# Retention and a gated MLP on one core: each chunk from the fifth on loaded as two halves instead of as one transfer

## The chip, the cores and the metric

The kernel runs on one core of a Trainium2 chip. The metric is the device time of one execution in microseconds (us), as the median of several runs. A core has TensorE (matmuls, PE in the profile, with its weight loads as PEld), VectorE (DVE), ScalarE (ACT), GpSimd (POOL) and SyncE (SP). Each works through its own queue of instructions in order; semaphores order them against each other. In this kernel SP computes nothing: it issues the transfers between memory (HBM) and the core's SBUF, which 16 DMA engines carry out.

## What is computed

There are 4 batches, 8 heads, 768 tokens and 64 values per head. For each batch and head a state of 64 x 64 decays at every token and takes up the product of k and v; the output is q times the state. Over the 512 joined head values of each token runs a gated MLP: a causal convolution of 5 taps gives a gate, the gate multiplies a projection, and a second projection follows.

```
for t in range(S):
    state = gamma * state + k[:, :, t] (outer) v[:, :, t]
    y[:, :, t] = scale * (q[:, :, t] . state)
x = y with the heads joined                     # (B, S, 512)
gate = sigmoid(sum over k of conv_w[k] * x shifted by k tokens)
out = (gate * (x @ w_val)) @ w_out
```

All of it is in 32-bit floating point; the weights come as 64-bit words that the kernel converts itself.

## The kernel before, in words

**Chunks.** The 768 tokens are cut into 6 chunks of 128. A chunk here is one chunk of tokens of one batch, with all heads, so there are 24, numbered 0 to 23 in the order of `chunks`: the four batches' first chunks are 0 to 3. In memory a chunk is 128 partitions of four planes of 512 values: plane 0 is q by dimension, plane 1 is k by dimension, plane 2 is v by token, plane 3 is k by token. For chunks 0 to 3 plane 3 is not loaded but made on the chip (`turn`, `take`). A whole chunk of four planes is 1 MB, with 8 KB per partition. The tile `att` that holds it has four buffers (`LB = 4`), so chunk g + 4 goes into the buffer of chunk g.

**Work on a chunk.** `decay` (GpSimd, line 192) multiplies v in place by its decay; for chunks 0 to 3 it does this to k. `scores` (TensorE, line 201) multiplies k and q by dimension into PSUM, `mask` (VectorE, line 210) masks them into u, `state` (TensorE, line 222) adds the products of k and v by token to the state, in two halves of 64 tokens, and `snap` (ScalarE, line 232) copies the state out. `y_scores` multiplies u with v and `y_state` the state with q (both at line 342), and `evac` (VectorE, line 395) scales the result into x. For chunks 4 to 23 TensorE's part is `block`, which takes up chunk g and begins chunk g + 1, in this order: `y_scores(g)`, `state(g, 1)`, `state(g + 1, 0)`, `y_state(g)`, `scores(g + 1)`. The first of it, `first_block`, is `state(4, 0)` and then `scores(4)`.

**The MLP.** Weights are converted on ScalarE, VectorE and GpSimd into a high and a low part. Of x, too, a rounded part (`round_x`, ScalarE) and its rest (`rest_x`, GpSimd, line 408) are made. `val` (TensorE, line 537) and `outp` (line 565) are the two projections, with three products each. `tap` (line 521 on ScalarE, line 523 on VectorE) is the convolution. `store` (ScalarE, line 575) copies a result out of PSUM, `send` (SP, line 579) writes it to memory.

**Order.** Every piece of work is a `Step` with its engine, what it reads and what it writes. `steps` are sorted by their due times, and the list `TURNS` gives the order in which they are written out, by number; -1 stands for `fill`, a matmul on zeros that keeps TensorE busy. `plan` asserts that no step comes ahead of what it needs and that a buffer's users are all written out ahead of the first user of the next tile in it. What an engine does in which order is fixed by that list; when it does it is up to the semaphores. The loads are steps too: `load_at` makes them and `load` issues them on SP (line 180), with the sends and the weight loads (line 423) in the same queue.

Of the kernel before, what the change touches and what calls it, by code (L numbers as in the profile page):

```python
# [16 lines left out]
P = 128  # L17
# [30 lines left out]
def plan(steps, turns, fill):  # L48

    steps = sorted(steps, key=lambda s: s.due)  # L50
# [36 lines left out]
    return [steps[i] if i >= 0 else fill for i in turns]  # L87
# [3 lines left out]
def tile_retention_gated_mlp(  # L91
# [70 lines left out]
    steps = []  # L162
# [143 lines left out]
    def fill():  # L306
        nc.tensor.matmul(
            z_ps[:, 0].rearrange("p b j e -> p (b j e)"),
            lhsT=warm.broadcast_to([P, P]), rhs=warm.broadcast_to([P, 512]),
            start=not begun, stop=True, skip_group_check=True,  # L310
        )
# [270 lines left out]
    def first_sigmoid():  # L582
# [345 lines left out]
    with tc.manual_schedule():  # L928
        for step in plan(steps, TURNS, Step(0.0, "PE", 0.2345, [], [], fill, ())):
            step.fn(*step.args)  # L930
# [99 lines left out]
```

## Time and profile before

| | |
|---|---|
| median of 3 runs | 213.23 us (213.15 to 213.98) |
| span of the profiled execution, first to last instruction | 212.0 us |
| TensorE busy | 202.8 us (96%), weight loads 160.9 us |
| VectorE, ScalarE, GpSimd busy | 136.0, 110.0, 105.6 us |
| SP's transfers | 34.66 MB on one queue, 44.0% of the 16 engines' span |
| loads of chunks | 20 of 1 MB, 3 of 768 KB, one in pieces of 512 and 256 KB |

The page gives no time of the profiled execution but its span; the median of the runs is 1.2 us more. [...] A row of a timeline gives the start of a group, how long it lasts from its first start to its last end, the engine, the line, the operation and the tiles; where the engine was idle ahead of it, the idle time and what ended it stand in brackets. Matmuls overlap in TensorE, so that a group's own duration is longer than the distance to the next group's start.

### The profile page before, as it was taken

What the parts mean: (1) busy time and instruction counts of PE and PEld (TensorE: products, weight loads), DVE (VectorE), ACT (ScalarE), POOL (GpSimd) and SP (SyncE); (2) the same over time, 40 slices, a digit from 0 to 9 for tenths busy, and PEclk for the clock granted to TensorE, in tenths of its full rate; (3) what the DMA queues carried; (4) which work ended last, traced back from release to release, by engine and by line L of the source; (5) the groups of instructions that cost most, each with busy time, mean ns of one, the idle gap of its engine ahead of it and who ended that gap; (6) DMA issues with size and microseconds to landing.
All of it is one profiled execution on the core that took longest, in us unless ns stands there. A gap on an engine that the chain in (4) does not pass through costs nothing.

```text
span 212.0 us, 7499 instructions
## 1 busy us (share of the span) xinstructions
PE 202.8 (96%) x3322; PEld 160.9 (76%) x3325; DVE 136.0 (64%) x209; ACT 110.0 (52%) x228; POOL 105.6 (50%) x98
## 2 busy tenths in 40 slices
PE   8999679999899999999999999999999999999993
PEld 3688467687687888888888878788878778877783
DVE  2986899999989952369736782616768257680000
ACT  2367988779835845273533742526560664523321
POOL 1277679899982337922239651422820456041300
PEclk9999999999999999999999999999999999999998
DMA  6998998576800995619533370111110111111122
GB/s 213 374 401 295 416 417 313 187 274 206 306 17 3 356 351 202 242 52 370 195 135 107 145 237 16 51 54 53 53 45 4 49 53 49 49 49 49 53 99 99
DMA packets 8402, 35.18 MB, mean 166 GB/s; under 512 B 937, under 2 KB 1193, under 8 KB 5810
## 3 DMA queue, kind: packets, MB, share of 16 engines
q1 hardware_dynamic: 8352, 34.66, 44.0%
q8 instruction: 26, 0.43, 0.8%
q10 hardware_dynamic: 18, 0.04, 0.1%
q14 instruction: 6, 0.05, 0.1%
HBM read 28.41 MB, written 6.29 MB: 164 GB/s over the span
## 4 chain that ended last, share of the span: by engine, by line
PE 82%; DVE 9%; ACT 2%; DMA 2%; issue 2%; SPq 0%; DVEq 0%; ACTq 0%
PE mm L565 32%; PE mm L537 28%; PE sy L342 9%; DVE acc L523 3%; PE sy L201 3%; PE z_ps L222 3%; PE sy L245 3%; DMA att<-in_att_dram 2%; PE mm L301 2%; PE mm L332 1%; PE z_ps L320 1%; DVE top L472 1%; DVE acc L478 1%; DVE acc L466 1%; DVE rest L482 1%
## 5 line engine op out<-in xcount | busy, mean ns | idle before, releaser
L523 DVE SCALAR_TENSOR_TENSOR acc<-x,cw_sb,acc 128x512 f32<-128x512 f32 x96 | 69.4, 751 | 7.2 <-ACT acc L521 6.4
L557 POOL TENSOR_TENSOR gvl<-gate,gvh 128x512 fp32r<-128x512 f32 x24 | 31.0, 1292 | 49.7 <-ACT gvh L553 49.6
L565 PE MATMUL mm<-woh,gvh 128*128 128x512 f32 (+1 forms) x100 | 38.9, 393 | 0.0
L575 ACT COPY o_sb<-mm 128x512 f32<-128x512 f32 (+1 forms) x25 | 14.2, 569 | 46.9 <-PE mm L565 46.8
L565 PE MATMUL mm<-wol,gvh 128*128 128x512 f32 (+1 forms) x100 | 38.5, 387 | 0.0
L565 PE MATMUL mm<-woh,gvl 128*128 128x512 f32 (+1 forms) x100 | 38.4, 386 | 0.0
L546 DVE TENSOR_TENSOR gate<-mm,gate 128x512 f32<-128x512 f32 x24 | 16.6, 690 | 33.0 <-PE mm L537 30.3
L408 POOL TENSOR_TENSOR xl<-x,xh 128x512 fp32r<-128x512 f32 x24 | 30.5, 1286 | 10.7 <-ACT xh L404 10.7
L192 POOL TENSOR_TENSOR att<-att,first_sb 128x512 f32<-128x512 f32 x24 | 24.9, 1042 | 19.2 <-DMA att<-in_att_dram 13.3
L537 PE MATMUL mm<-xh,wvh 128*128 128x512 f32 x96 | 32.5, 413 | 1.4 <-ACT xh L404 1.0
L537 PE MATMUL mm<-xh,wvl 128*128 128x512 f32 x96 | 30.3, 399 | 0.8 <-issue 0.8
L537 PE MATMUL mm<-xl,wvh 128*128 128x512 f32 x96 | 30.3, 397 | 0.5 <-POOL xl L408 0.5
L530 ACT ACTIVATE gate<-acc 128x512 f32<-128x512 f32 x24 | 14.3, 597 | 17.3 <-DVE acc L523 11.1
L565 PEld LDWEIGHTS mm<-woh,gvh 128*128 128x128 f32 x100 | 18.7, 188 | 5.4 <-ACT o_sb L575 1.3
L537 PEld LDWEIGHTS mm<-xh,wvl 128*128 128x128 f32 x96 | 18.0, 188 | 5.6 <-issue 1.1
L537 PEld LDWEIGHTS mm<-xh,wvh 128*128 128x128 f32 x96 | 17.4, 188 | 6.3 <-ACT xh L404 1.1
L565 PEld LDWEIGHTS mm<-woh,gvl 128*128 128x128 f32 x100 | 18.8, 188 | 4.0
L537 PEld LDWEIGHTS mm<-xl,wvh 128*128 128x128 f32 x96 | 17.8, 188 | 5.1 <-POOL xl L408 1.2
L565 PEld LDWEIGHTS mm<-wol,gvh 128*128 128x128 f32 x100 | 18.8, 188 | 3.7
L395 DVE TENSOR_TENSOR x<-sy,dec 128x512 f32<-128x512 f32 x20 | 13.8, 688 | 10.3 <-PE sy L201 9.6
L553 ACT CAST gvh<-gate 128x512 fp32r<-128x512 f32 x24 | 14.9, 619 | 6.9 <-DVE gate L546 4.4
L232 ACT COPY snap<-z_ps 128x256 f32<-128x256 f32 x40 | 14.7, 373 | 6.2 <-PE z_ps L222 4.8
(65 smaller groups left out, 268.9 us busy)
## 6 DMA issues: line engine op xcount, KB each, us to landing
att<-in_att_dram SPq DMA_DIRECT2D x20, 1024.0 KB, 6.5
out_dram<-o_sb SPq DMA_DIRECT2D x23, 256.0 KB, 2.1
wst<-in_w_dram SPq DMA_DIRECT2D x7, 512.0 KB, 7.9
att<-in_att_dram SPq DMA_DIRECT2D x3, 768.0 KB, 8.9
first_sb<-in_first_dram SPq DMA_DIRECT2D x1, 568.0 KB, 3.7
att<-in_att_dram SPq DMA_DIRECT2D x1, 512.0 KB, 5.0
att<-in_att_dram SPq DMA_DIRECT2D x1, 256.0 KB, 6.7
out_dram<-o_sb SPq DMA_DIRECT2D x2, 128.0 KB, 1.8
```

The source lines that it names most:

```text
L192: nc.gpsimd.tensor_tensor(v, v, vd_sb[:, c, :].unsqueeze(2).broadcast_to([P, 8, HALF]), op=ALU.mult)
L232: nc.scalar.copy(sn, z_ps[:, :, b])
L342: return nc.tensor.matmul(sy[cols, h, off:off + HALF], lhsT=lhsT, rhs=rhs, start=start, stop=True, skip_group_check=True,)
L408: nc.gpsimd.tensor_tensor(xl[n, ct], xs[n][:, ct, :, HALO:], xh[n, ct].bitcast(F32), op=ALU.subtract)
L523: nc.vector.scalar_tensor_tensor(acc, x[:, :, k:k + P], cw_sb[:, m, k:k + 1], acc, op0=ALU.mult, op1=ALU.add,)
L530: nc.scalar.activation(gate[n, m], accs.pop((n, m)), AF.Sigmoid)
L537: nc.tensor.matmul(vps[n, m], lhsT=w[:, m, ct * P:(ct + 1) * P], rhs=xx[n, ct].rearrange("p b t -> p (b t)"), start=(i == 0), stop=(i == 3 ...
L546: nc.vector.tensor_tensor(gv, vps.pop((n, m)), gv, op=ALU.mult)
L553: nc.scalar.copy(gvs[n, m][0], gate[n, m])
L557: nc.gpsimd.tensor_tensor(gvl, gate.pop((n, m)), gvh.bitcast(F32), op=ALU.subtract)
L565: nc.tensor.matmul(ops[n, b, cs.start][:, 0:cs.stop - cs.start], lhsT=gg[:, b * P:(b + 1) * P], rhs=w[:, ct, cs], start=(i == 0), stop=(i ...
L575: nc.scalar.copy(o_sb[:, 0:step], ops.pop((n, b, cs.start))[:, 0:step])
```

## The change

A chunk of four planes, from chunk 4 on, is loaded by two transfers of 512 KB instead of one of 1 MB. The first brings planes 0 and 1 (q and k by dimension), the second planes 2 and 3 (v and k by token). On SP the second stands right behind the first. Each has a step of its own: the first writes what `scores` and `y_state` read, the second what `decay`, `state` and `y_scores` read. There are 20 steps more, so the numbers in `TURNS` change, and the list is written anew. Read out engine by engine, the new list has the order of the old one on TensorE, VectorE, ScalarE and GpSimd, with all 17 fillers in their places; on SP it has the old order with each chunk's load replaced by its two halves. `fill` gets a size, and a second, smaller filler (128 columns) is made that the list does not use.

```diff
-def plan(steps, turns, fill):
+def plan(steps, turns, fills):
...
-    return [steps[i] if i >= 0 else fill for i in turns]
+    return [steps[i] if i >= 0 else fills[-1 - i] for i in turns]
...
-    def fill():
+    def fill(size):
         nc.tensor.matmul(
-            z_ps[:, 0].rearrange("p b j e -> p (b j e)"),
-            lhsT=warm.broadcast_to([P, P]), rhs=warm.broadcast_to([P, 512]),
+            z_ps[:, 0].rearrange("p b j e -> p (b j e)")[:, 0:size],
+            lhsT=warm.broadcast_to([P, P]), rhs=warm.broadcast_to([P, size]),
             start=not begun, stop=True, skip_group_check=True,
         )
...
     TURNS = (
...
     )
...
-        pieces = PIECES_OF.get(g, ((0, 4 if g >= B else 3),))
+        pieces = PIECES_OF.get(g, ((0, 2), (2, 4)) if g >= B else ((0, 3),))
         for a, z in pieces[1:] if late else pieces[:1] if (2, g) in FIRST_LOADS else pieces:
             what = [k for k, i in zip(keys, (1, 2, 3)) if a <= i < z]
             at(due, "DMA", 0.63 * (z - a), [], what, load, g, slice(a, z))
...
-        for step in plan(steps, TURNS, Step(0.0, "PE", 0.2345, [], [], fill, ())):
+        for step in plan(steps, TURNS, [Step(0.0, "PE", 0.2345, [], [], fill, (n,)) for n in (512, 128)]):
             step.fn(*step.args)
```

## Rows read from the trace of the kernel before

**Rows 1.** The page, part 1: busy us of each engine (share of span), instructions.

```profile
PE 202.8 (96%) x3322; PEld 160.9 (76%) x3325; DVE 136.0 (64%) x209; ACT 110.0 (52%) x228; POOL 105.6 (50%) x98
```

**Rows 2.** The page, part 4: the chain that ended last, shares of the span.

```profile
PE 82%; DVE 9%; ACT 2%; DMA 2%; issue 2%; SPq 0%; DVEq 0%; ACTq 0%
```

**Rows 3.** That chain in order of time, 20 to 30 us: start, us, what.

```profile
25.71 0.60 ACT acc L521
...
26.34 0.76 DVE acc L523
```

**Rows 4.** The table of waits: who waited for whom, us in total, times, longest.

```profile
POOL att L192 <- DMA att<-in_att_dram: 13.3, 6, 4.7
...
PEld z_ps L222 <- POOL att L192: 1.0, 1, 1.0
...
PE mm L537 <- POOL xl L408: 0.5, 1, 0.5
```

**Rows 5.** Loads of `att` on SP: issue ns; chunk 4's landing; timeline.

```profile
L180 SPq DMA_DIRECT2D att<-in_att_dram x25: 327/328/1208, 1.2 to 122.0; - x25
...
DMA to landing us min/median/max: 6.6/6.6/6.6
...
15.69 2.91 SPq L180 DMA_DIRECT2D att<-in_att_dram  x2
```

**Rows 6.** Timeline of GpSimd: the decays of chunks 4, 5, 6 with 7, and 14.

```profile
22.51 1.04 POOL L192 TENSOR_TENSOR att<-att,first_sb 128x512 f32<-128x512 f32 x1 [0.76 <-DMA att<-in_att_dram]
...
25.59 1.05 POOL L192 TENSOR_TENSOR att<-att,first_sb 128x512 f32<-128x512 f32 x1
...
32.76 2.04 POOL L192 TENSOR_TENSOR att<-att,first_sb 128x512 f32<-128x512 f32 x2
...
73.73 1.04 POOL L192 TENSOR_TENSOR att<-att,first_sb 128x512 f32<-128x512 f32 x1 [3.43 <-DMA att<-in_att_dram]
```

**Rows 7.** Timeline of TensorE, 22 to 27 us: state and scores of chunk 4, first projection.

```profile
23.60 0.46 PE L222 MATMUL z_ps<-att 64*64 64x64 f32 x16 [0.72 <-POOL att L192]
23.88 0.65 PE L201 MATMUL sy<-att 64*64 64x64 f32 x32
25.49 0.50 PE L537 MATMUL mm<-xh,wvh 128*128 128x512 f32 x1 [0.96 <-ACT xh L404]
```

**Rows 8.** One stretch: its length, busy us by engine, granted clock, DMA share, GB/s.

```profile
21.20:31.80 10.60, 7.44 (x221) 5.73 (x219) 9.92 (x16) 9.41 (x21) 7.87 (x10) 1.00 1.02 416
```

**Rows 9.** Timeline of VectorE: chunk 4's mask and the tap behind it.

```profile
24.80 0.69 DVE L210 TENSOR_TENSOR u<-sy,tri_sb 128x512 f32<-128x512 f32 x1
...
26.34 0.76 DVE L523 SCALAR_TENSOR_TENSOR acc<-x,cw_sb,acc 128x512 f32<-128x512 f32 x1 [0.26 <-ACT acc L521]
```

**Rows 10.** Timeline of TensorE: the state matmuls of chunks 13 and 14.

```profile
76.74 0.65 PE L222 MATMUL z_ps<-att 64*64 64x64 f32 x32
```

**Rows 11.** Line 222: wait instructions on TensorE's queue, whole span, then 48.9 to 49.2 us.

```profile
L222 PEldq EVENT_SEMAPHORE  x16: 51/51/164, 22.3 to 149.1; - x16
...
L222 PEldq EVENT_SEMAPHORE  x1: 51/51/51, 49.0 to 49.0; - x1
```

**Rows 12.** Timeline of TensorE: state, product with the state and scores in one block.

```profile
49.04 0.65 PE L222 MATMUL z_ps<-att 64*64 64x64 f32 x32
49.50 0.65 PE L342 MATMUL sy<-att,snap 64*64 64x64 f32 x32
49.97 0.65 PE L201 MATMUL sy<-att 64*64 64x64 f32 x32
```

**Rows 13.** The page, part 6: the stores, KB each, median us from issue to landing.

```profile
out_dram<-o_sb SPq DMA_DIRECT2D x23, 256.0 KB, 2.1
...
out_dram<-o_sb SPq DMA_DIRECT2D x2, 128.0 KB, 1.8
```

**Rows 14.** SP's timeline and `att` landings, 22.5 to 24 us: chunk 7's load.

```profile
22.96 0.33 SPq L180 DMA_DIRECT2D att<-in_att_dram  x1
...
DMA to landing us min/median/max: 9.4/9.4/9.4
```

132 rows, old and new, of the table TURNS are left out of this document.

## The prediction

> **What bounds the kernel now.** I read the busy shares first [rows 1], then the chain that ended last, first by engine and then in order of time [rows 2, 3], then the waits that a load can cause [rows 4], and last the neighbourhood of each such wait on SP, PE, VectorE and GpSimd. The reader is to see in the first that TensorE is busy for 202.8 of 212.0 us, so that all its idle time is 9.2 us; in the second that 82% of the chain is TensorE and 9% VectorE, and that only 2% is a transfer. That 2% is the very first load, of chunk 0, which the change leaves alone. In the third the reader is to see that after the first four chunks the chain goes to ScalarE and VectorE (25.71 to 26.34 us here) and not through a transfer or GpSimd: the transfers of chunks 4 to 23 are nowhere on it.
>
> The waits say the same in another way. GpSimd's decay of v waits six times for a landing, 13.3 us in all, but TensorE has waited for a decay in the blocks only once, for 1.0 us on its weight side [rows 4]. So five of the six waits on GpSimd are spare time of GpSimd. The one that reaches TensorE is chunk 4's: SP issues that load at 15.69 us, it lands 6.6 us later, at 22.3 [rows 5]; the decay starts at 22.51 and takes 1.04 [rows 6]; TensorE starts the state of chunk 4 at 23.60 after 0.72 idle [rows 7].
>
> **Part 1: who reads the first half.** The first half (q and k by dimension) is read by the scores and by the product of q with the state; the second (v and k by token) by the decay, the state and the product of v. In a block the first state of the next chunk stands ahead of its scores on TensorE, and in the first block too. So for every one of the 20 chunks the second half is wanted before the first, and a first half that lands early (by about half of the transfer) is waited for by nobody. The worth of the earlier landing is 0 us. What matters is when the second half lands, compared with the whole chunk before.
>
> **Part 2: the second half's landing.** SP issues 20 transfers more. An issue takes 0.33 us (0.327 smallest, 0.328 median, 1.208 largest) [rows 5], so the second half is asked for some 0.38 us later than the whole was: one issue and the small gap behind it. The bytes are the same. Between 21.2 and 31.8 us, with loads queued one behind the other, the 16 DMA engines have a busy share of 1.02 and move 416 GB/s [rows 8]: no gap shows between one queued transfer and the next, and 512 KB take 0.524 / 416 = 1.3 us (an estimate from that row). The first half's 1.3 us therefore cover the 0.38 us, and the second half should land when the whole did. The ends are 0 and 0.38 us of lateness where the cover holds; if the issue were as slow as the slowest one seen, 1.2 us. Earlier by up to 1.3 us is possible only if the first half is asked for earlier (the third rival). I take 0.1 us.
>
> What does lateness cost? At chunk 4 the decay and the state move with it at once: the state starts 0.05 us after the decay's end (22.51 + 1.04 = 23.55, against 23.60). Then there is slack. Its scores end at 23.88 + 0.65 = 24.53 and VectorE's mask starts only at 24.80, since VectorE is busy: 0.27 us. Behind the mask VectorE has 0.26 us idle before the tap at 26.34, which waits for ScalarE [rows 9]. TensorE itself next waits 0.96 us for ScalarE [rows 7]. So 0.27 + 0.26 = 0.53 us of lateness are absorbed at chunk 4 before the chain moves, and 0.1 or 0.38 us cost nothing. With 1.2 us it would cost 1.2 - 0.53 = 0.7 us. Of the other chunks whose decay waits for a landing, chunk 14 is the tightest: its decay starts at 73.73 [rows 6] and ends at 74.77, and the state is in the block whose state matmuls start at 76.74 [rows 10], 2.0 us later. Chunk 5's decay, at 25.59, waits for no landing.
>
> **Part 3: SP's queue.** Behind each load on SP stand other loads, weight loads and sends. Each is pushed back by 0.38 us per split load ahead of it, where SP is not waiting anyway. SP mostly waits: for TensorE to free a buffer, or for ScalarE's result. The largest pile is where three chunks are asked for behind the first send, 3 x 0.38 = 1.1 us for the send behind them; in the table of waits no row of TensorE, ScalarE or VectorE names a store. Without that cover a send could at most be 1.1 us late in mid-kernel; the sends at the end have no load ahead of them. Cost 0.
>
> **Part 4: one wait more per chunk on TensorE.** The scores now read data that no earlier instruction of TensorE has waited for, so each of 20 scores gains a wait that is long satisfied. The nearest row is the wait for a load ahead of the state: 16 separate wait instructions on TensorE's queue, 51 ns in the median [rows 11]. At one end each is paid in full, 20 x 0.051 = 1.0 us; at the other nothing. One of them, at 49.0 us, stands among the state's 32 matmuls of that block, and these take 49.50 - 49.04 = 0.46 us, while the next 32, with none, take 49.97 - 49.50 = 0.47 [rows 12]. So it is hidden by the matmuls in flight, and I take 0 to 0.01 us each, 0.1 us in all. The orders on TensorE, VectorE, ScalarE and GpSimd stay as they were, and the new size of the filler is never used, so the rewritten list by itself costs 0.
>
> **The sum.** 0 (part 1) + 0 (part 2, 0.1 us of lateness under 0.53 of slack) + 0 (part 3) + 0.1 (part 4) on the profiled execution's span of 212.0 us gives 212.1. The runs shown have a median of 213.23, 1.2 us more than that span; with the same 1.2 us around it, 213.3. That is the forecast; its own range is 212.9 to 213.9, and the change would not be visible: about 0.5% (1.07 us) is what a measurement of this kernel can tell from no change.
>
> **Rivals.** (1) *Each half pays a start of its own, and the second lands late (slower).* Stores of 128 and 256 KB land after 1.8 and 2.1 us [rows 13]: 0.3 us for the second 128 KB, so some 1.5 us of start (estimate). If that were not overlapped, chunk 4 would cost 1.5 - 0.53 = 0.97 us, 214.2. Four split loads follow each other there, and the lateness L of each adds up to chunk 7, which lands at 22.96 + 9.4 = 32.4 [rows 14]; its decay is the second of two from 32.76, so from 33.8 [rows 6], 1.4 us later. Late by 4 x 1.5 - 1.4 = 4.6 us it holds up the rounding remainders behind it on GpSimd, for which TensorE already waits 0.5 us [rows 4]: 217.9. It decides from 4L - 1.4 = 1.07, L = 0.6 us. Against it: the busy share of 1.02 [rows 8]. Chance 0.06. [...]
>
> (2) *The added waits are paid:* 1.0 us, 214.3. For it: TensorE has little idle time to hide them in. Against it: the 0.46 us above. Chance 0.05.
>
> (3) *The halves are freed apart (faster).* If the first half's buffer counts as free once the scores have read it, SP can ask for it earlier, and chunk 4's second half lands up to 1.3 us sooner. TensorE's wait there, 0.7 to 1.0 us, goes. But TensorE then waits longer for ScalarE, and the mask is held by VectorE; most likely nothing comes of it, 213.2. At the other end 1.0 us is gained, 212.2. Chance 0.07, for which nothing in this trace speaks directly.
>
> **The numbers.** Forecast 0.82; rivals 0.06, 0.05 and 0.07. Faster by over 0.5% lies at the far end of rival 3: 0.05. Slower by over 0.5% is rival 1 and a little of rival 2: 0.08. Within 0.5%: 0.87. The range, 212.5 to 214.2, takes in the 0.8 us between the runs shown, the 0.7 us of a slow issue and most of rivals 2 and 3, and leaves out rival 1's larger end.
>
> **What would show it.** Right: the 20 chunks stand as 40 issues of 512 KB; the second half of chunk 4 lands at 22.2 to 22.7; TensorE's wait for the decay there stays near 0.7 to 1.0 us; the four orders repeat nearly to the tenth; TensorE's busy time stays near 202.8. Wrong in part 2: chunk 4's decay starts after 23.0, or TensorE waits for a decay in more places than one. Wrong in part 4: the 32 scores take over 0.5 us. Rival 3: a first half is issued well before 15.69. What would make the whole wrong is a consumer that I have not seen to wait for q and k.

## The result and the profile after

| | before | after |
|---|---|---|
| median | 213.19 us (6 runs, 212.79 to 213.98) | 215.31 us (6 runs, 214.55 to 215.69) |
| ratio, 95% interval | | 1.0087 [1.0066, 1.0109] |
| profiled execution, span | 212.0 us | 212.8 us |
| granted clock, mean | 0.997 | 0.981 |

The change costs 2.1 us (0.9%), where I had said that it would not be seen. Time less span is 1.66 to 1.80 us in all executions of all kernels here, so the loss lies inside the span. The profiled execution of after is the fastest of its six runs (212.8 + 1.75 = 214.55), and it shows only part of the loss.

The page of after, the parts that answer to [rows 1, 2, 5]: busy us, queues, the chain by engine, loads with KB each and median us to landing.

```profile
PE 201.6 (95%) x3323; PEld 160.5 (75%) x3325; DVE 135.9 (64%) x209; ACT 109.6 (51%) x228; POOL 105.7 (50%) x98
...
q1 hardware_dynamic: 11232, 34.67, 46.3%
q8 instruction: 26, 0.43, 0.8%
...
PE 80%; DVE 6%; DMA 5%; issue 3%; ACT 2%; SPq 1%; POOL 1%; ACTq 0%
...
att<-in_att_dram SPq DMA_DIRECT2D x41, 512.0 KB, 5.7
```

The reader is to see that no engine works more, that the chain has 3% "issue" (2% before), and a queue that I had passed over: q8, "instruction", 26 packets with 0.43 MB, 16 KB each. It stands in the page of before with the same numbers. The chain's 5% DMA (2% before) is not the split loads here: it is one piece of 9.9 us that begins at 3.97 us, before the first of them is issued.

TensorE's timeline in after, three of the places where it stops:

```profile
25.15 0.49 PE L537 MATMUL mm<-xh,wvh 128*128 128x512 f32 x1 [1.63 <-ACT xh L404]
...
29.41 0.28 PE L222 MATMUL z_ps<-att 64*64 64x64 f32 x3 [2.25 <-issue]
...
57.98 0.50 PE L537 MATMUL mm<-xh,wvl 128*128 128x512 f32 x1 [0.73 <-issue]
```

The same view of before, two rows that front and prediction do not have:

```profile
28.38 0.28 PE L222 MATMUL z_ps<-att 64*64 64x64 f32 x3 [0.86 <-issue]
...
57.00 0.50 PE L537 MATMUL mm<-xh,wvl 128*128 128x512 f32 x1 [0.81 <-issue]
```

The stops marked "issue" wait for no tile and no semaphore that the profile shows. They stand in both kernels at the same instruction. (The stop of 1.63 us in after waits for ScalarE, as the one of 0.96 us does in [rows 7].)

GpSimd's timeline in after, the decays of chunks 4 to 7 and what follows them (compare [rows 6]):

```profile
21.49 1.04 POOL L192 TENSOR_TENSOR att<-att,first_sb 128x512 f32<-128x512 f32 x1
...
25.25 1.06 POOL L192 TENSOR_TENSOR att<-att,first_sb 128x512 f32<-128x512 f32 x1
...
32.38 1.06 POOL L192 TENSOR_TENSOR att<-att,first_sb 128x512 f32<-128x512 f32 x1
33.84 1.04 POOL L192 TENSOR_TENSOR att<-att,first_sb 128x512 f32<-128x512 f32 x1 [0.40 <-DMA att<-in_att_dram]
34.84 3.77 POOL L408 TENSOR_TENSOR xl<-x,xh 128x512 fp32r<-128x512 f32 x3
```

Chunk 4's decay waits for no landing and starts 1.0 us earlier than in before. That is not the change's doing: in the control below, the kernel before run again (e0), it starts at 21.50 us. But the decays of chunks 6 and 7, which were one group of two in [rows 6], are torn apart: chunk 7's second half is late, and the three rounding remainders (L408) start behind it.

### The profile page after: what moved, and what is told of

Its sections match the earlier page's. It is cut to its first block, busy times and chain, and to the rows that moved or that the text cites. A ratio compares the mean times of both kernels' runs of the same rounds, so it can differ in the third digit from the quotient of the medians.

```text
span 212.8 us, 7529 instructions
## 1 busy us (share of the span) xinstructions
PE 201.6 (95%) x3323; PEld 160.5 (75%) x3325; DVE 135.9 (64%) x209; ACT 109.6 (51%) x228; POOL 105.7 (50%) x98
## 3 DMA queue, kind: packets, MB, share of 16 engines
q1 hardware_dynamic: 11232, 34.67, 46.3%
## 4 chain that ended last, share of the span: by engine, by line
PE 80%; DVE 6%; DMA 5%; issue 3%; ACT 2%; SPq 1%; POOL 1%; ACTq 0%
PE mm L565 32%; PE mm L537 29%; PE sy L342 8%; DMA att<-in_att_dram 5%; PE sy L201 3%; PE z_ps L222 3%; DVE acc L523 1%; PE z_ps L320 1%; PE sy L245 1%; SPq L180 1%; DVE gate L546 1%; PE mm L301 1%; DVE x L395 1%; DVE u L210 1%; DVE top L472 1%
## 5 line engine op out<-in xcount | busy, mean ns | idle before, releaser
L408 POOL TENSOR_TENSOR xl<-x,xh 128x512 fp32r<-128x512 f32 x24 | 30.5, 1288 | 10.5 <-ACT xh L404 10.5
L537 PE MATMUL mm<-xh,wvh 128*128 128x512 f32 x96 | 33.2, 424 | 1.6 <-ACT xh L404 1.6
L537 PE MATMUL mm<-xh,wvl 128*128 128x512 f32 x96 | 30.9, 405 | 0.7 <-issue 0.7
L537 PEld LDWEIGHTS mm<-xh,wvh 128*128 128x128 f32 x96 | 18.1, 195 | 6.3 <-ACT xh L404 1.8
L537 PEld LDWEIGHTS mm<-xh,wvl 128*128 128x128 f32 x96 | 18.5, 192 | 5.4 <-issue 1.0
```

The costliest lines, as they stand in the source:

```text
L408: nc.gpsimd.tensor_tensor(xl[n, ct], xs[n][:, ct, :, HALO:], xh[n, ct].bitcast(F32), op=ALU.subtract)
L537: nc.tensor.matmul(vps[n, m], lhsT=w[:, m, ct * P:(ct + 1) * P], rhs=xx[n, ct].rearrange("p b t -> p (b t)"), start=(i == 0), stop=(i == 3 ...
```

## Experiments

All kernels are the kernel before with the edit shown, so that its line numbers hold. Most change only line 180, where SP issues a load; only e8 to e10 and e12 to e14 touch what TensorE issues. The medians of the kernel before that were measured beside them are 213.15 to 213.32 us. Below, "the code theory" means: TensorE's program comes in pieces of 16 KB (the 26 packets of q8, whose time the page counts on the same 16 DMA engines as the loads', 0.8% of their span), and a piece that is asked for behind queued loads comes late.

### e0 and e1: the control, and the halves alone

e0 is the kernel before, unchanged.

> The kernel before, unchanged, as a control. Both theories: ratio 1.000, within 0.2%. The code-block theory: TensorE's stop in the middle of the state matmuls of chunk 5, put down to issue (0.86 us in the profile of before), lasts 0.5 to 1.2 us here too, since the 16 KB block of TensorE's code that it waits for is fetched behind the loads in flight from 21 us on.

Measured: 213.5 us, ratio 1.0025 [1.0005, 1.0045]. The same kernel differs from itself by a quarter of a per cent; smaller differences below carry no weight. In its traced execution TensorE has one "issue" stop, at 57 us:

```profile
56.53 0.50 PE L537 MATMUL mm<-xh,wvl 128*128 128x512 f32 x1 [0.68 <-issue]
```

The stop near 28 us, expected to last 0.5 to 1.2 us, is not there: a miss. It comes and goes between executions of the same kernel.

```diff
# e1
-        nc.sync.dma_start(out=tiles[g][:, part], in_=att[i, :, part])
+        [nc.sync.dma_start(out=tiles[g][:, a], in_=att[i, :, a])
+         for a in ((slice(0, 2), slice(2, 4)) if g >= B else (part,))]
```

> The kernel before with its old list, in which each load from chunk 4 on issues two halves: the change without the rewritten list. Code-block theory and the theory of a cost per added transfer: as slow as the changed kernel, ratio 1.007 to 1.011. A theory that the rewritten list costs something: 1.000. Code-block theory: the stop in the state of chunk 5 lasts over 1.8 us.

Measured: 215.22 us, 1.0101 [1.0083, 1.012], as after. So the loss is made by the two transfers; the new list, the steps of their own and the finer waits add nothing to it. Its stop near 28 us lasted 0.54 us, not over 1.8: a second miss on that stop. Its profiled execution, 215.98 us, is the slowest of its five and shows the loss at 105 us, which after's, the fastest of six, does not have; TensorE in e1:

```profile
58.37 0.50 PE L537 MATMUL mm<-xh,wvl 128*128 128x512 f32 x1 [0.81 <-issue]
...
106.32 0.40 PE L565 MATMUL mm<-wol,gvh 128*128 128x512 f32 x1 [0.82 <-issue]
```

and GpSimd in e1:

```profile
32.62 1.06 POOL L192 TENSOR_TENSOR att<-att,first_sb 128x512 f32<-128x512 f32 x1
34.89 1.04 POOL L192 TENSOR_TENSOR att<-att,first_sb 128x512 f32<-128x512 f32 x1 [1.21 <-DMA att<-in_att_dram]
```

Here the chain that ended last (start, us, what) runs through chunk 7's second half, its decay and the remainders, which in before it did not:

```profile
23.37 11.38 DMA att<-in_att_dram
...
34.89 1.04 POOL att L192
35.94 3.73 POOL xl L408 x3
```

### e2 and e3: early chunks, late chunks

```diff
# e2: 4 <= g <= 8;  e3: g >= 9
-((slice(0, 2), slice(2, 4)) if g >= B else (part,))
+((slice(0, 2), slice(2, 4)) if 4 <= g <= 8 else (part,))
```

> Halves for chunks 4 to 8 alone, which are issued between 15 and 31 us. Code-block theory (the late fetch of one block at 27 us, and the clock that falls behind it): nearly the whole loss, ratio 1.006 to 1.011, stop over 1.8 us. Theory of a cost per added transfer, evenly over the 20 (a wait on TensorE, an issue on SP, or something outside the span): 5/20 of it, about 1.002.

> Halves for chunks 9 to 23 alone, issued from 35 us on, after the stop. Code-block theory: ratio 0.999 to 1.002 and a stop of 0.5 to 1.2 us as before. Theory of a cost per added transfer: 15/20 of the loss, about 1.0065.

Measured: e2 214.01 us, 1.0035 [1.001, 1.006]; e3 214.77 us, 1.0077 [1.0049, 1.0106]. My first form of the code theory put nearly all the loss at the stop near 28 us; it fell (that stop is 0.82 us in e2, not over 1.8). Five early chunks carry about a third of the loss, fifteen later ones the rest, which is nearer to the theory of an even cost per transfer (1.002 and 1.0065). e3, whose early chunks are whole, even has a stop of 1.70 us near 29 us in its trace and is level with before again by 34 us.

### e4 and e5: the chunks whose loads stand ahead of a code stop

Ahead of the stop at 57 us the loads of chunks 12 and 13 are in the queue (in before issued at 50.3 and 53.9 us and landed 4.8 and 6.9 us later), ahead of that at 105 us those of 19 and 20 (94.3 and 94.8, 5.5 and 8.6). e4 splits these and, besides, 22.

```diff
# e4: g in (12, 13, 19, 20, 22);  e5: the other 15
-if g >= B else (part,)
+if g in (12, 13, 19, 20, 22) else (part,)
```

> Halves for chunks 12, 13, 19, 20 and 22 alone, whose loads are in flight when TensorE asks for the code blocks that it waits for at 57 and at 105 us. Theory A (the loss comes from those two stops on code blocks, longer behind halves): 1.004 to 1.008, with a stop of over 1.0 us at 57 and one of 0.5 us or more at 105. Theory B (a cost per added transfer, wherever it is): 5 of 20 transfers, 1.0025.

> Halves for all chunks from 4 on but 12, 13, 19, 20 and 22. Theory A: 1.001 to 1.004, the stop at 57 us as before (0.7 to 0.8) and none at 105. Theory B: 15 of 20 transfers, 1.0075.

Measured: e4 214.12 us, 1.0026 [1.0002, 1.005]; e5 214.13 us, 1.0036 [1.0014, 1.0059]. TensorE in e4:

```profile
57.57 0.50 PE L537 MATMUL mm<-xh,wvl 128*128 128x512 f32 x1 [1.34 <-issue]
...
105.36 0.39 PE L565 MATMUL mm<-wol,gvh 128*128 128x512 f32 x1 [0.69 <-issue]
```

and in e5:

```profile
56.80 0.50 PE L537 MATMUL mm<-xh,wvl 128*128 128x512 f32 x1 [0.23 <-issue]
```

with none at 105. So in these traces the five chunks make the stops at 57 and 105 us long, and the other fifteen do not; e3, which splits the five, has 1.15 and 0.57 us there, e2, which does not, 0.76 and none. The medians, each within the control's 0.25% of the other, could not have told that: e4's lies where an even cost per transfer puts it (1.0025) and under what the code theory said (1.004 to 1.008), e5's where the code theory puts it and not at 1.0075.

### e6 and e7: what of a half costs, its size or its rows

```diff
# e6: halves by partition, whole rows of 8 KB
+        [nc.sync.dma_start(out=tiles[g][r, part], in_=att[i, r, part])
+         for r in ((LO, HI) if g >= B else (slice(0, P),))]
# e7: one transfer of 1 MB, from a copy in memory with the halves apart: rows of 4 KB
+        nc.sync.dma_start(
+            out=tiles[g][:, part] if g < B else tiles[g].rearrange("p (h a) x j n -> p h (a x j n)", h=2),
+            in_=att[i, :, part] if g < B else rows4[i].rearrange("h p n -> p h n"))
```

> Two transfers of 512 KB per chunk as in the change, but cut by partitions (64 and 64), so that each row stays 8 KB. If the number of transfers costs: 1.007 to 1.011, as the change. If the shorter rows (4 KB instead of 8) cost: 0.998 to 1.003.

> One transfer of 1 MB per chunk as before, but from a copy in memory whose two halves lie apart, so that each row is 4 KB instead of 8. If the shorter rows cost: 1.007 to 1.011, as the change, and the queue's share of the 16 engines goes from 44.0% to 46.3%. If the number of transfers costs: 0.998 to 1.003.

Measured: e7 213.26 us, 1.000 [0.9978, 1.0023], with 10912 packets on q1 (8352 before, 11232 after). The shorter rows and the larger number of packets cost nothing here (ratio 1.000); the second transfer does (e1, 1.0101). e6 took 240.1 us (1.12), outside both expectations, and tells nothing of halves, since its transfers to 64 partitions each moved 215 GB/s from 16 to 24 us, against 372 in e7 (last section).

### e8, e9, e10: moving TensorE's code instead of the loads

If a late piece of code is the cause, the place where the program is cut into pieces must matter, with no load touched. Leaving out a filler (two instructions) moves every later cut.

```diff
# e8 (from e1) and e9 (from before): five of the -1 in TURNS out, those at 26 to 38 us
-        ... 98, -1, 105, 137, -1, 166, ... 138, -1, 152, ... 204, -1, 240, ... 195, -1, 189, ...
+        ... 98, 105, 137, 166, ... 138, 152, ... 204, 240, ... 195, 189, ...
# e10 (from before): twelve fillers of 64 columns ahead of the first data
+            if n == 2:
+                [fill(64) for _ in range(12)]
```

> Chunks 4 to 23 in halves, as in e1, but five fillers (10 of TensorE's instructions, those at about 26 to 38 us) are left out, so every later piece of TensorE's code begins 10 instructions further on and is asked for that much earlier against the time it is needed. If the halves cost what they do because a piece of TensorE's code comes late behind them (needed at 57 us and at 105 us), about 1 us more of lead at 57 and 0.6 us at 105 takes most of both stops away: the stop at 57 falls from 0.81 us in e1 to under 0.4 us, that at 105 from 0.82 to under 0.3, and the time from 215.2 us to 213.3 to 214.2. If the halves cost by themselves (late data, a later decay, a longer queue on SP), nothing of this moves and it stays at 214.7 to 215.4 us.

> The kernel before with the same five fillers left out, one load per chunk. By the code theory the stop of 0.7 us at 57 us goes and the time falls to 212.4 to 212.9 us (from 213.2). If the stop is something else, 213.0 to 213.4 us. Left out fillers could also let the clock drop between 26 and 38 us, which the granted clock would show.

> The kernel before, one load per chunk, with 12 more fillers of 64 columns (24 instructions) ahead of the first data, while TensorE has nothing else to do: no load, no step and no order changes, only where TensorE's code is cut into pieces. By the code theory the pieces needed near 54 and 101 us are now asked for just as two loads stand in the queue, with 3 us of lead instead of 4.6 and 5.8: new stops put down to issue of 1 to 3 us each there, together 2 to 5 us, so 215 to 218 us. If code has no part in it, 213.2 us with an uncertainty of 0.4.

Measured: e10 217.6 us, 1.0178 [1.0135, 1.022]: 24 instructions with next to no work, at a time when TensorE waits for data anyway, cost 4.4 us with every load whole. TensorE in e10:

```profile
51.16 1.33 PE L537 MATMUL mm<-xl,wvh 128*128 128x512 f32 x5 [0.49 <-issue]
...
56.69 0.34 PE L201 MATMUL sy<-att 64*64 64x64 f32 x5 [2.20 <-issue]
...
104.75 0.39 PE L537 MATMUL mm<-xh,wvh 128*128 128x512 f32 x1 [1.86 <-issue]
```

The stops sit on other instructions than before (scores, the next product), and two of them are over twice as long as any in before. That is what the code theory said of e10 (215 to 218 us), without the change. Counting makes it firmer. In before's trace TensorE has 6675 instructions (weight loads, matmuls and waits) for the 26 packets of q8, 257 to a packet, and the first two stops of e10 named below stand 257 instructions apart; I count 256 to a piece. Numbered in the order of the trace, the instructions behind the stops are 704 and 2239 in before, 705, 2242 and 4545 in e1, 1981, 2238 and 4541 in e10. All stand 189 to 194 behind a multiple of 256, whatever they compute, and so does every "issue" stop after 12 us in all kernels here but one of 0.36 us near 26 us in e11 to e13. e8: 214.29 us, 1.004 [1.0019, 1.0061], 0.9 us less than e1 and 0.1 over what I expected; the stop at 57 us is 0.37 us, at 105 there is none. e9: 213.25 us, 1.0002 [0.9987, 1.0016]: the stop at 57 us is gone as expected, the time is not, a miss. Its profiled execution has this instead:

```profile
28.83 0.36 PE L222 MATMUL z_ps<-att 64*64 64x64 f32 x2 [2.06 <-issue]
```

and from 25 to 35 us a granted clock of 0.68 and 0.64. Whether the fillers taken out there are its cause was not settled; e12 has 0.66 from 25 to 30 us with those fillers in place. Halves still cost 1.0 us over whole loads (e8 against e9), so the code stops were not all of it.

### e11 to e14: the late half, and both causes apart

The trace of e8 still had GpSimd waiting 1.21 us for chunk 7. So e11 keeps all 40 transfers but asks for v and k by token first. e12 and e13 cut the code 12 instructions later by leaving out six fillers of the first 11 us, so that the middle keeps its own. e14 is e13 with the order of the change.

```diff
# e11 (from e1)
-((slice(0, 2), slice(2, 4)) if g >= B else (part,))
+((slice(2, 4), slice(0, 2)) if g >= B else (part,))
# e12 (from before), e13 (from e11), e14 (from e1)
-        ... 14, -1, 16, -1, 15, -1, 19, -1, 18, 8, 17, 7, 10, -1, 20, -1, 28, ... 25, -1, 35, 34, -1, 37, ...
+        ... 14, -1, 16, 15, 19, 18, 8, 17, 7, 10, -1, 20, 28, ... 25, 35, 34, 37, ...
```

> All chunks 4 to 23 in halves as in e1, but the half with v and k by token is asked for first, the half with q and k by dimension behind it. Two theories of the early half of the loss (about 1 us, lost between 33 and 39 us in the traces of e1, e2, e5 and e8): (i) chunk 7's second half lands late and GpSimd's decay of it waits, so that the rounding remainders behind it come late; then the half that the decay reads now lands a half earlier, the decay of chunk 7 starts at 33.3 to 33.9 us as it does with whole loads (34.1 to 35.0 in those runs), TensorE no longer waits twice for xl near 38 us, and only the stops at 57 and 105 us remain: 213.9 to 214.5 us. (ii) the loss is of the second transfer by itself, whatever it carries: 215.2 us as in e1. A new loss would show where the scores wait for their half.

> The kernel before, one load per chunk, with six fillers (12 instructions) left out of the first 11 us instead of five out of the middle as in e9. The code pieces behind it are cut 12 instructions later, so the stop at 57 us should go as in e9, and the fillers of 26 to 38 us that keep TensorE's clock stay: 212.4 to 213.0 us, under both kernels. If TensorE's clock falls in the first 11 us for want of the six, it is 213.2 to 214.

> e11 and e12 together: halves with v and k by token first, and TensorE's code cut 12 instructions later. If the two causes are all there is (the late half of chunk 7, the code pieces at 57 and 105 us), the 20 transfers more now cost next to nothing: 212.6 to 213.4 us, within 0.4 us of e12. If they cost by themselves, 1 us or more over e12.

> The halves in the order of the change (q and k by dimension first) with TensorE's code cut 12 instructions later, as in e13. If the two causes are separate, the stops at 57 and 105 us are away and only the late half of chunk 7 is left: its decay starts at 34 to 35 us instead of about 33.1, TensorE waits for xl more than once near 38 us, and the time lies about 0.5 to 1.1 us over e13's 212.85: 213.4 to 214.0 us. If the late half costs only together with the code pieces, it is 212.9 us like e12 and e13.

Measured, medians with the ratio to before:

| | one load of 1 MB | halves, q and k first | halves, v and k first |
|---|---|---|---|
| code as in before | 213.15 | 215.22 (e1), 1.0101 [1.0083, 1.012] | 214.41 (e11), 1.0056 [1.0034, 1.0077] |
| code 12 instructions later | 212.90 (e12), 0.9992 [0.9974, 1.001] | 214.10 (e14), 1.003 [1.0013, 1.0046] | 212.85 (e13), 0.9993 [0.9974, 1.0012] |

Forty transfers cost nothing (e13 against e12) once the half that is wanted first is asked for first and the code stops are moved. Each cause alone is seen too: e11 has the code stops at 57 and 105 us and no late half, e14 the late half and no stop at 57 or 105. e14's median lies 0.1 us over what I expected, the others within it. The clock that e12's expectation puts down to the fillers of 26 to 38 us was 0.66 from 25 to 30 us in e12, with them in place, and 1.00 from 0 to 15 us without the six. GpSimd in e13, back to one group of two:

```profile
32.12 2.04 POOL L192 TENSOR_TENSOR att<-att,first_sb 128x512 f32<-128x512 f32 x2
34.13 3.77 POOL L408 TENSOR_TENSOR xl<-x,xh 128x512 fp32r<-128x512 f32 x3
```

GpSimd in e14, torn apart again:

```profile
32.22 1.06 POOL L192 TENSOR_TENSOR att<-att,first_sb 128x512 f32<-128x512 f32 x1
34.36 1.04 POOL L192 TENSOR_TENSOR att<-att,first_sb 128x512 f32<-128x512 f32 x1 [1.09 <-DMA att<-in_att_dram]
35.36 3.76 POOL L408 TENSOR_TENSOR xl<-x,xh 128x512 fp32r<-128x512 f32 x3
```

TensorE in e14, one wait for the remainders more than e13 has:

```profile
37.95 0.73 PE L537 MATMUL mm<-xl,wvh 128*128 128x512 f32 x2 [0.51 <-POOL xl L408]
39.18 0.73 PE L537 MATMUL mm<-xl,wvh 128*128 128x512 f32 x2 [0.50 <-POOL xl L408]
```

Chunk 7's is not the only late half. Chunk 10's decay, in e13 and then in e14:

```profile
50.68 1.03 POOL L192 TENSOR_TENSOR att<-att,first_sb 128x512 f32<-128x512 f32 x1
...
52.24 1.04 POOL L192 TENSOR_TENSOR att<-att,first_sb 128x512 f32<-128x512 f32 x1 [0.56 <-PE mm L537]
```

The view names TensorE, but in e14 the half that this decay reads was issued at 46.03 us and landed 6.1 us later, just ahead of the decay; in after, e1 and e5 the decay waits 0.41 to 0.54 us in the same way. No run parts this half from chunk 7's: e11 and e13 put both right.

TensorE in e11, the code stops that are left:

```profile
56.68 0.50 PE L537 MATMUL mm<-xh,wvl 128*128 128x512 f32 x1 [1.00 <-issue]
...
104.57 0.40 PE L565 MATMUL mm<-wol,gvh 128*128 128x512 f32 x1 [0.79 <-issue]
```

Where the time goes along the span, worked out from the traces: how much later than in e0 (whose stop at 57 us is 0.68 us) the same instruction starts, in us.

```
place (its time in e0)      before  after    e1    e11    e12    e13    e14    e10
y_scores(5), 33.64            0.32   1.98   1.64  -0.16  -0.28  -0.29  -0.18  -0.04
y_scores(6), 38.90            0.33   1.15   1.47  -0.16  -0.28  -0.30   0.94  -0.05
y_scores(9), 51.89            0.33   1.00   1.25  -0.18  -0.28  -0.24   0.71   0.52
y_scores(10), 60.00           0.47   1.45   1.84   0.12  -0.57  -0.53   1.02   2.02
val, 100.70                   0.47   1.46   1.85   0.13  -0.54  -0.54   1.06   4.05
val, 123.04                   0.47   1.46   2.83   1.07  -0.54  -0.54   1.06   4.05
outp, 206.62                  0.45   1.42   2.85   1.07  -0.54  -0.51   1.02   4.01
```

e1 loses 1.3 us by 52 us, 0.6 more by 60 and 1.0 at 105. Not all of the 0.6 is code: e14, which has no stop at 57, goes from 0.95 us behind e13 to 1.55 over the same stretch, just behind chunk 10's late half, while e1's stop there is only 0.13 us longer than e0's. The table on top says the same in medians: the order of the halves is worth 0.8 us (e1 to e11) and 1.25 (e14 to e13), the code's position 1.1 (e1 to e14) and 1.6 (e11 to e13). e12 and e13 lie 0.3 us under before, less than these runs can tell from no change, so I name no version that beats both.

**Why a piece of code comes late.** The trace has the start of each q8 packet. Counting 256 instructions to a piece, the wait from TensorE's entry into the piece before to the start of the packet for the piece needed at 105 us is 2.8 to 3.2 us where chunks 19 and 20 are whole (before, e0, e2, e5, e7), and 4.2 to 4.8 where they are halves (e1, e3, e4, e8, e11, e13, e14); in after's profiled execution it happened to be 2.2, and there was no stop. From one entry to the next it has 5.9 us in before's trace. The packet itself takes about 1 us (0.88 to 1.53 in before), and TensorE went on 1.2 to 1.5 us after its end wherever it stopped at such an edge. With these added, 2.8 to 3.2 us fit into 5.9 and 4.2 to 4.8 do not. In e13 and e14, cut 12 instructions later, the same stretch has 7.3 us, and there is no stop. The longest stop at such an edge here is the 2.25 us near 29 us in after.

**Why chunk 7's second half comes late.** The stretch in which chunks 4 to 7 are loaded, 16 to 24 us: busy us by engine, clock, DMA share, GB/s. Before:

```profile
16.00:24.00 8.00, 7.28 (x154) 6.35 (x154) 5.68 (x12) 6.68 (x15) 5.26 (x8) 1.00 0.91 336
```

After:

```profile
16.00:24.00 8.00, 7.46 (x172) 6.39 (x168) 6.02 (x13) 6.70 (x16) 4.97 (x7) 1.00 0.98 322
```

e1:

```profile
16.00:24.00 8.00, 6.75 (x128) 5.82 (x127) 5.81 (x12) 6.69 (x15) 5.11 (x8) 1.00 0.79 226
```

e7, one transfer with the same short rows:

```profile
16.00:24.00 8.00, 7.42 (x170) 6.35 (x167) 6.06 (x13) 7.12 (x16) 5.24 (x9) 1.00 0.98 372
```

The kernels with whole loads move 336 to 372 GB/s there (before, e0, e3, e4, e7, e9, e10, e12), those with halves 224 to 322 (after, e1, e2, e5, e8, e11, e13, e14). Against e0's 360, e1 is short of (0.360 - 0.226) x 8 = 1.07 MB, which at 416 GB/s [rows 8] is 2.6 us. In e11 and e13 the stretch is just as slow (308, 297), but what is late there is q and k, which nobody wants yet. Why the engines move less is not shown: neither the rows (e7) nor the bytes, nor a later issue of the loads on SP, explains it, and no run here changed only the number of transfers in flight.

## Why the prediction was wrong

**Part 1 held.** Nobody waits for the first half. e13 is the proof from the other side: q and k may land last at no cost.

**Part 2 failed, at chunk 7.** At chunk 4, which I had worked through, it held in after: the second half landed at 21.2 us, the whole in e0 at 21.1, and the decay started without a wait. (In e1, e8 and e14 chunk 4's decay waited 0.70 to 1.28 us, but with whole loads it waited 0.76 in before and 1.40 in e4; in none of these did it start after 23.0.) The step that failed is "the first half's 1.3 us therefore cover the 0.38 us". It took the rate of [rows 8], 416 GB/s with the queue full from 21 us on, for the stretch before, in which SP still feeds the queue load by load and whole loads reach 336 to 372. The lateness then adds up to chunk 7, which landed at 33.7 us in after and 34.8 in e1 against 32.0 in e0, and whose decay waited 0.40 us in after and 0.65 to 1.21 in e1, e2, e5, e8 and e14, where I had bounded a half's lateness at 0.38 us. (In e4, whose early loads are whole, it waited 0.69 us in the profiled execution, and in before, e0, e7, e9 and e12 not at all: the margin there is thin.) That is rival 1, by its own formula: 4L - 1.4 = 0.4 to 1.2 gives L = 0.45 to 0.65, around the 0.6 that I gave as the point from which it decides. I gave it 0.06 because the row that spoke against it was read from the wrong stretch. I also took only chunks whose decay waits for a landing in before, and so missed chunk 10: there the whole landed at 49.9 us and the decay started at 51.25 (1.35 us of slack), which the second half used up. The 1.5 us of start that I estimated from the stores [rows 13] is more than twice the L found here. Whether L is what is left of such a start is not shown.

**A term was missing: TensorE's code.** I asked who reads the chunk, and listed decay, scores, state and the two products. What the prediction called "a consumer that I have not seen" reads none of it: it is the program of TensorE, on a queue beside the loads. It could have been read from before: two stops of 0.86 and 0.81 us put down to "issue", 2% "issue" in the chain [rows 2], and the queue q8 on the page. Such a stop can be a wait without slack: at 57 us e11's is 0.32 us longer than e0's, and e11 loses 0.30 us there and 0.95 at 105. It need not be: e3's 1.70 us near 29 us left it only 0.28 us behind e0 at 34. I passed over these two because no tile's name stood in them. Moving the code gave 1.1 to 1.6 us with halves and 0.25 with whole loads (before to e12, not told from no change), so the change's share is some 0.9 to 1.3 us.

**Parts 3 and 4 held.** If SP's longer queue or the added waits cost anything, e13 would show it against e12, with all 20 transfers more; the medians are 212.85 and 212.90. The finer waits are in after and not in e1, and these agree within 0.1 us; after's trace has 16 separate wait instructions at the state, as before, and none at the scores. Rival 2 did not come. Nor did rival 3: the first halves were asked for when the buffer came free (15.35 us in after, the whole at 15.25 in e0), and no wait was saved.

**The sum.** 0.1 us in place of 2.1: late halves 0.8 to 1.25, code 0.9 to 1.3, the larger of one with the smaller of the other, together 2.1 (e1 less before). I also put 1.2 us around the span; it is 1.7, since before's profiled execution was 0.5 us slower than its median, whose span is 211.5.

## What to carry to other kernels

Before moving or splitting transfers, look for stops that the trace puts down to "issue": they can be the engine's own code waiting behind loads, a consumer that may have no slack (here up to 2.25 us in one stop, and 0.95 us lost to the stop of 0.79 at 105 us in e11). Where loads are split, ask first for the half that is wanted first (worth 0.8 and 1.25 us here), and read the rate of transfers from the stretch in which the queue is being filled, not from the one in which it is full (336 to 372 GB/s for whole loads here, against 416). Where the program is cut into pieces is part of a schedule: 24 instructions more, at the start of e10, made a stop of 2.20 us near 57 us and one of 1.86 near 105.

## What the hardware showed that I had not expected

**Code position.** 24 instructions more at the start cost 4.4 us (e10), 12 less gave back 1.6 us with halves (e11 to e13) and 0.25 with whole loads (before to e12), the latter within the control's difference.

**Transfers to 64 partitions.** e6 loads the same bytes with rows of 8 KB by two transfers to 64 partitions each. The stretch from 16 to 24 us in e6:

```profile
16.00:24.00 8.00, 6.43 (x122) 5.49 (x118) 6.12 (x13) 6.64 (x16) 3.92 (x6) 1.00 1.01 215
```

All engines are busy (1.01) and move 215 GB/s, against 372 for e7 at 0.98; the kernel takes 240 us. Why is not shown.

**The clock between 25 and 35 us.** The stop of 2.25 us in after ends at 29.41 us; the granted clock (the third number from the end) around it:

```profile
25.00:30.00 5.00, 2.45 (x100) 1.91 (x104) 4.65 (x8) 4.21 (x11) 3.90 (x5) 1.00 0.98 357
30.00:35.00 5.00, 5.00 (x57) 4.02 (x50) 4.90 (x9) 4.46 (x9) 4.60 (x5) 0.66 1.03 404
```

0.66 is the mean of the stretch: microsecond by microsecond the granted clock is 0.90, 0.50, 0.50, 0.50 and 0.89. TensorE, busy throughout, does 57 matmuls there. With VectorE at 4.90 of 5 us in the same stretch, how much of it was paid is not separated from the late half. A long stop ahead of it is not the rule: e3 and e5 stop for 1.70 and 1.41 us and stay at 1.00, and e12 and e13, the two fastest kernels here, have 0.66 from 25 to 30 us with no stop over 0.36.
